# Attention with a gated convolution: the row of reciprocals turned by VectorE, another start and another end

## The chip, the core and the metric

The kernel runs on one core of a Trainium2 chip. The metric is the time on the device, in microseconds (us), of one execution; the kernel before was timed in three runs. A core has five engines that work from queues of their own and wait for each other by semaphores: TensorE (PE, matrix products; its weight loads are listed as PEld), VectorE (DVE), ScalarE (ACT), GpSimd (POOL) and SyncE (SP), which in this kernel issues every DMA transfer. Matrix products land in PSUM, everything else lies in SBUF.

## The reference, cut to what matters

```python
# B, C = 4, 128; 384 x 32 positions, so N = 12288 queries per batch
kv_pool = kv.reshape(B, H // 4, 4, W // 4, 4, C).mean(axis=(2, 4))   # 768 keys per batch
k = v = kv_pool.reshape(B, -1, C) @ w_sr
s = (q @ k.transpose(0, 2, 1)) / sqrt(C)
a = exp(s - s.max(-1));  a /= a.sum(-1) + 1e-09
x = a @ v                                                            # (B, N, C)
gate = sigmoid(sum_k conv_w[k] * xp[:, k:k + N])                     # five causal taps along N
out = (gate * (x @ w_val)) @ w_out
```

The weights `w_val`, `w_out` and `conv_w` arrive as float64 and are turned into float32 on the chip.

## The kernel before, in words

The queries are cut into groups of 512 (`GQ`), 24 for a batch and 96 in all, and a group into four tiles of 128 queries (`NT = 4`). The keys of a batch come in 16 pieces of 384 KB; a piece holds the 16 values that belong to each of 48 keys (`PC = 48`), and `pool_kv` sums them with one `tensor_reduce` on VectorE. Five buffers hold pieces (`AHEAD = 5`).

A tile's work is one step `t` of the main loop, in a hand-written order (the program switches its scheduler to manual, so each engine's instructions stand as the code is written). `score` forms 128 x 768 scores as three products for each half of the keys, with keys and queries split into a high and a low part (`kh`, `kl`, `qh`, `ql`), one tile ahead and in one of three pairs of PSUM banks. `row_max` (VectorE), `expo` (ScalarE, which also sums the row into column `j` of the tile `z`), `p_hi` (ScalarE) and one step later `p_lo` (VectorE) make a high and a low half-precision part of the probabilities. `p_lo` frees the bank pair. In most tiles a DMA transpose (`pt<-hl`) turns the parts; in a group's last tile, TensorE turns them (`turn`, L299). The last batch turns every tile of its even groups by DMA. Two groups later `av_part` multiplies them with the values: 18 products for a group, 7, 2, 3 and 6 in its four steps. `g_x` (VectorE) scales the result with the row of 1/z, which has been spread over all partitions (`rb`), and writes `x`. GpSimd makes four of the convolution's taps and adds them up (`g_conv`, L360 and L369), also subtracts for `ql` (L237), and copies the four values that the next group's `x` needs from the one before (L346). `g_tanh`, `g_val`, `g_h`, `g_out` and `g_evac` finish a group three and more groups behind.

The row of 1/z comes about so. `z` is a 128 x 128 tile of zeros with four columns in use. `norm_reciprocal` (L276, VectorE) inverts the four columns in step `j == 0` of the next group. `norm_turn` (L279) turns the whole tile by a TensorE transpose into the one bank `misc()`. In step `j == 1`, `norm_store` copies four rows of it to SBUF (L286, VectorE) and SP stores these 2 KB to DRAM (`rd<-r`, L287). At the end of step `j == 3`, `norm_rows` (L292) reads them back, broadcast over 128 partitions (`rb<-rd`). `g_x` uses `rb` one group later.

Before the loop stand the loads and sums of the first batch's keys, two projections by `w_sr` (L133, half of the keys each), and the scores of one tile. The weights' load (`load_moe`) is issued after the ninth piece, and its 14 VectorE instructions are strewn over the loop's steps from `t = 3`. Behind the loop stands the end, for the last groups `n1` (the last) to `n5`: `n2` and `n1` are convolved by VectorE alone (`conv_dve`), `n1` in two halves of 256 columns.

## Time and profile before

| | before |
|---|---|
| median of 3 runs | 1077.52 us (1075.18 to 1078.14) |
| profiled execution | 1078.68 us, of which the profile's span is 1076.9 us |
| mean granted TensorE clock | 0.996 |
| busy, us | PE 1038.4, PEld 706.5, DVE 919.5, ACT 903.7, POOL 865.2 |
| chain that ended last | PE 89%, DVE 5%, ACT 2%, DMA 2% |
| DMA queues | 92.7% of 16 engines' span, 220.25 MB |

The span begins with the first instruction on the core and ends with the last; some 2 us of the execution lie outside it. A busy share is a mean over the whole span, and the first 50 us and the last 25 us differ from the middle. A row of the timeline gives start, duration, engine, line, operation, what is written from what is read, and in brackets the idle time before it with what ended it. On SP the duration is that of issuing a transfer, not of its landing.

### The profile page before, as it was taken

The page shows a single profiled execution, that of the slowest core. Times are in us where ns is not written, and L with a number is a line of the kernel's source. Part 1 is how long each engine was busy: PE and PEld are TensorE (multiplying, and loading weights), DVE is VectorE, ACT ScalarE, POOL GpSimd, SP SyncE. Part 2 cuts the span into 40 slices and gives each one's busy share as a digit, 9 for nine tenths or more (in the row PEclk, how much of TensorE's full clock was granted, in tenths as well). Part 3 has the DMA queues.
Part 4 walks back from the last instruction along what each step waited for, and adds up shares of the span by engine and source line. Part 5 has one row for each costly group of instructions (what it writes and reads, how often), then busy time and mean ns, then how long its engine had stood idle before and what let it go on. Part 6 is the DMA issues. An engine that isn't in the chain of part 4 may idle for free.

```text
span 1076.9 us, 16475 instructions
## 1 busy us (share of the span) xinstructions
PE 1038.4 (96%) x5102; PEld 706.5 (66%) x5102; DVE 919.5 (85%) x1290; ACT 903.7 (84%) x1659; POOL 865.2 (80%) x948
## 2 busy tenths in 40 slices
PE   1899999999999999999999999999999999999996
PEld 0666666666666666666676666666666666666663
DVE  6888989898888898988888989898888888888885
ACT  1788888888888888888888888888888988888882
POOL 0178888888888888888888888888887888888882
PEclk9999999999999999999999999999999999999999
DMA  7699999998889999999689999997899999999994
GB/s 285 115 237 215 214 225 234 200 192 190 182 186 234 226 222 224 220 214 188 156 182 221 248 216 219 235 218 177 174 203 191 200 209 218 206 194 212 201 178 120
DMA packets 505527, 220.25 MB, mean 205 GB/s; under 512 B 471520, under 2 KB 472288, under 8 KB 505440
## 3 DMA queue, kind: packets, MB, share of 16 engines
q1 hardware_dynamic: 505440, 219.20, 92.7%
q8 instruction: 41, 0.67, 0.2%
q14 instruction: 46, 0.38, 0.1%
HBM read 75.83 MB, written 25.36 MB: 94 GB/s over the span
## 4 chain that ended last, share of the span: by engine, by line
PE 89%; DVE 5%; ACT 2%; DMA 2%; issue 1%; POOL 0%; SPq 0%; DVEq 0%; ACTq 0%
PE s L251 36%; PE av L333 32%; PE m L389 7%; PE m L399 7%; PE s L299 5%; DMA kvt<-in_kv 2%; DVE nm L257 1%; PE m L279 1%; ACT s L269 1%; ACT hl L316 1%; DVE hl L320 1%; DVE pt L320 1%; DVE pool L120 0%; DVE x L350 0%; PE m L176 0%
## 5 line engine op out<-in xcount | busy, mean ns | idle before, releaser
L333 PE MATMUL av<-pt,vh 128*128 128x512 f16 x1140 | 387.1, 381 | 0.0
L369 POOL TENSOR_TENSOR sum<-sum,tap 128x512 f32<-128x512 f32 x282 | 360.3, 1278 | 22.1
L257 DVE TENSOR_REDUCE nm<-s 128x1 f32<-128x768 f32 x384 | 363.9, 948 | 2.8 <-PE s L251 2.8
L269 ACT ACTIVATE s<-s,nm 128x768 f32<-128x768 f32 x300 | 262.0, 873 | 88.7 <-DVE nm L257 80.0
L360 POOL TENSOR_SCALAR tap<-x,wm 128x512 f32<-128x512 f32 x376 | 253.4, 693 | 78.1 <-DVE x L350 76.8
L320 DVE SCALAR_TENSOR_TENSOR hl<-s,hl 128x768 f16<-128x768 f32 x300 | 284.8, 949 | 21.4 <-ACT hl L316 21.1
L251 PE MATMUL s<-kh,qh 128*128 128x384 f32 x768 | 252.9, 410 | 6.0 <-DVE hl L320 2.3
L316 ACT ACTIVATE hl<-s 128x768 f16<-128x768 f32 x300 | 243.0, 810 | 9.1
L333 PEld LDWEIGHTS <-vh 128*128 128x128 f16 x1164 | 113.5, 98 | 173.6 <-issue 81.5
L333 PE MATMUL av<-pt,vl 128*128 128x512 f16 x570 | 216.0, 379 | 0.0
L251 PE MATMUL s<-kh,ql 128*128 128x384 f32 x768 | 198.0, 339 | 0.0
L251 PE MATMUL s<-kl,qh 128*128 128x384 f32 x768 | 197.7, 338 | 0.0
L237 POOL TENSOR_TENSOR ql<-q,qh 128x512 fp32r<-128x512 f32 x96 | 122.0, 1271 | 93.3 <-ACT qh L233 92.5
L251 PEld LDWEIGHTS s<-kh,qh 128*128 128x128 f32 x768 | 132.4, 192 | 51.1 <-PE m L279 4.4
L251 PEld LDWEIGHTS s<-kl,qh 128*128 128x128 f32 x768 | 140.5, 189 | 0.5 <-DVE kl L146 0.5
L251 PEld LDWEIGHTS s<-kh,ql 128*128 128x128 f32 x768 | 139.8, 189 | 0.0
L394 DVE SCALAR_TENSOR_TENSOR h<-th,m 128x512 f32<-128x512 f32 x94 | 64.7, 688 | 69.0 <-PE m L389 63.4
L369 POOL TENSOR_TENSOR sum<-tap,tap 128x512 f32<-128x512 f32 x94 | 120.3, 1280 | 0.0
L350 DVE SCALAR_TENSOR_TENSOR x<-av,down,rb 128x512 f32<-128x512 f32 x95 | 71.3, 751 | 44.5 <-POOL ql L237 30.5
L333 PEld LDWEIGHTS <-vl 128*128 128x128 f16 x582 | 57.2, 98 | 76.6 <-issue 53.6
L399 PE MATMUL m<-h,wm 128*128 128x512 f32 x188 | 96.8, 597 | 1.2 <-DVE h L394 1.2
L389 PE MATMUL m<-x,wm 128*128 128x512 f32 x188 | 96.1, 592 | 0.0
(68 smaller groups left out, 1001.9 us busy)
## 6 DMA issues: line engine op xcount, KB each, us to landing
kvt<-in_kv SPq DMA_DIRECT2D x64, 384.0 KB
rb<-rd SPq DMA_DIRECT2D x96, 256.0 KB
q<-in_q SPq DMA_DIRECT2D x47, 512.0 KB
out<-o SPq DMA_DIRECT2D x46, 512.0 KB
pt<-hl SPq DMA_TRANSPOSE x192
rd<-r SPq DMA_DIRECT2D x96, 2.0 KB
out<-o SPq DMA_DIRECT2D x3, 256.0 KB
q<-in_q SPq DMA_DIRECT2D x2, 256.0 KB
```

The lines of the kernel that those rows point to most:

```text
L237: nc.gpsimd.tensor_tensor(out=g.ql, in0=g.q, in1=g.qh.bitcast(F32), op=ALU.subtract)
L251: nc.tensor.matmul(s[:, h, :HALF], a[:, sl], k[:, h * HALF:(h + 1) * HALF], start=(i == 0), stop=(i == 2))
L257: nc.vector.tensor_reduce(out=nm, in_=g.s[j], axis=AX.XY, op=ALU.max, negate=True)
L269: nc.scalar.activation(out=halves(g.pf[j]) if on_pe(g, j) else g.s[j], in_=g.s[j], func=AF.Exp, bias=g.nm.pop(j), accum_out=g.z[:, j:j + 1])
L316: nc.scalar.activation(out=part(g, j, 0), in_=g.s[j], func=AF.Copy, scale=2.0 ** 15)
L320: nc.vector.scalar_tensor_tensor(out=part(g, j, 1), in0=g.s.pop(j), scalar=2.0 ** 15, in1=part(g, j, 0), op0=ALU.mult, op1=ALU.subtract)
L333: nc.tensor.matmul(out, g.st[v][:, k * P:(k + 1) * P], g.pt[:, j0:j1, a * NCH + k], start=(i == 0), stop=(i == len(AV_ORDER) - 1))
L350: nc.vector.scalar_tensor_tensor(out=g.x[:, HALO + c0:HALO + c1], in0=av, scalar=g.st["down"], in1=g.rb[:, c0:c1], op0=ALU.mult, op1=ALU.mult)
L360: eng.tensor_scalar(out=g.tap[k], in0=src, scalar1=w, scalar2=1.0, op0=ALU.mult, op1=ALU.mult)
L369: nc.gpsimd.tensor_tensor(out=s, in0=acc, in1=g.tap[k], op=ALU.add)
L389: nc.tensor.matmul(m, wval, g.x[:, HALO + c0:HALO + c1], start=True, stop=True)
L399: nc.tensor.matmul(m, wout, h, start=True, stop=True)
```

## The change: what it does

Three things change.

1. **The row of 1/z.** `norm_turn` leaves TensorE. VectorE turns four blocks of 32 x 32 of `z` (now 128 x 32) straight into the SBUF tile `r`, 32 x 128, of which four rows are stored as before; the copy out of PSUM goes. Reciprocal, four transposes and the store now stand together in step `j == 0`, behind `p_lo(prev)`; the reciprocal stood ahead of it. The broadcast read `norm_rows` stands in step `j == 2` ahead of `p_lo(prev)`, where it stood at the end of step `j == 3`.
2. **The start.** The weights are loaded first of all and converted at once. Pieces 0, 2, 4, 6, 8 and 10 are summed by GpSimd in four halvings (`pool_halving`). The keys are projected in three parts (keys 0 to 383, 384 to 671, 672 to 767), and the scores of tiles 0, 1 and 2 against the first half of the keys are written ahead of the second projection, their other half behind the last.
3. **The end.** `conv_mixed` gives two of the five taps to ScalarE; the order of the last groups' products is another, and PSUM banks are used in pairs.

```diff
-    zs = [const.tile([P, P], F32, name=f"z{i}") for i in range(3)]
+    zs = [const.tile([P, BLOCK], F32, name=f"z{i}") for i in range(3)]
...
+    def pool_halving(st, i):
+        t = st.pop(("kv", i)).rearrange("c (k s) -> c k s", s=RR)
+        n = RR // 2
+        while n:
+            if n == 1:
+                to = st["pool"][:, i * PC:(i + 1) * PC].rearrange("c (k s) -> c k s", s=1)
+            else:
+                to = kvp.tile([C, PC, n], F32, name=f"half{n}", bufs=1)
+            nc.gpsimd.tensor_tensor(out=to, in0=t[:, :, :n], in1=t[:, :, n:2 * n], op=ALU.add)
+            t, n = to, n // 2
...
-    def norm_turn(g, m):
-        nc.tensor.transpose(m[:, :P], g.z, ident)
-        g.rm = m[:NT, :P]
+    def norm_turn(g):
+        g.r = small.tile([BLOCK, P], F32, name="r")
+        for i in range(0, P, BLOCK):
+            nc.vector.transpose(out=g.r[:, i:i + BLOCK], in_=g.z[i:i + BLOCK])
...
-        nc.vector.tensor_copy(out=r, in_=g.rm)
-        nc.sync.dma_start(out=g.rd, in_=r)
+        nc.sync.dma_start(out=g.rd, in_=g.r[:NT])
...
+        late = [product(k) for k in range(TAPS - 2, TAPS)]
         s = work.tile([C, GQ], F32, name="fast")[:, :c1 - c0]
         nc.vector.tensor_scalar_mul(out=s, in0=g.x[:, c0:c1], scalar1=cwt[:, 0:1])
-        for k in range(1, TAPS):
+        for k in range(1, TAPS - 2):
...
+        for t in late:
+            nc.vector.tensor_tensor(out=s, in0=s, in1=t, op=ALU.add)
...
+    convert = load_moe()
     for i in range(AHEAD):
         load_kv(0, st, i)
...
+    by_pool = (1, 3, 5, 7, 9, 11)
+    ends = {PIECES // 2: slice(0, HALF), PIECES - 2: slice(HALF, NK - 2 * PC),
+            PIECES: slice(NK - 2 * PC, NK)}
+    for step in convert:
+        step()
+    for i in range(1, PIECES + 1):
+        (pool_halving if i in by_pool else pool_kv)(st, i - 1)
...
+        if low and (i == PIECES - 1 or i == PIECES - 3):
+            low()
+        if i in ends:
+            project(st, ends[i], misc())
+            high, low = split_keys(st, ends[i])
+            high()
+        if i == PIECES - 3:
+            for j in first:
+                score(at(0), j, (0,))
...
-        if last and j == 0:
-            norm_reciprocal(last)
-        if last and j == 1:
-            norm_store(last)
+        if last and j == 2:
+            norm_rows(last)
         drip()
         if prev:
             p_lo(prev, (j - 1) % NT)
...
         if last and j == 0:
-            norm_turn(last, misc())
+            norm_reciprocal(last)
+            norm_turn(last)
+            norm_store(last)
...
-        if last and j == 3:
-            norm_rows(last)
```

Three places show what moves. The first is VectorE's queue in the middle of the program, from a group's `g_x` (`x<-av,down,rb`) to the next group's `h`; `nm` is the row maximum, `pt` and `hl` are the results of `p_lo`, `z_102` one of the three `z`. Before:

```order
L350 SCALAR_TENSOR_TENSOR x<-av,down,rb 128x512
L257 TENSOR_REDUCE nm<-s 128x1
L276 RECIPROCAL z_102<-z_102 128x4
L320 SCALAR_TENSOR_TENSOR pt<-s,pt 128x768
L257 TENSOR_REDUCE nm<-s 128x1
L286 COPY r<-m 4x128
L320 SCALAR_TENSOR_TENSOR hl<-s,hl 128x768
L394 SCALAR_TENSOR_TENSOR h<-th,m 128x512
```

Now:

```order
L364 SCALAR_TENSOR_TENSOR x<-av,down,rb 128x512
L271 TENSOR_REDUCE nm<-s 128x1
L334 SCALAR_TENSOR_TENSOR pt<-s,pt 128x768
L290 RECIPROCAL z_102<-z_102 128x4
L296 STREAM_TRANSPOSE r<-z_102 32x32 x4
L271 TENSOR_REDUCE nm<-s 128x1
L334 SCALAR_TENSOR_TENSOR hl<-s,hl 128x768
L419 SCALAR_TENSOR_TENSOR h<-th,m 128x512
```

Reciprocal and transposes stand between `p_lo` of the last group's last tile and the row maximum of the group's second tile; the copy is gone.

The second is SP's queue for one group in the same stage, from its DMA transposes on. Before:

```order
L324 DMA_TRANSPOSE pt<-hl 128x24x128
L324 DMA_TRANSPOSE pt<-hl 128x12x128
L292 DMA rb<-rd 128x512
L117 DMA kvt<-in_kv 128x768
L413 DMA out<-o 128x1024
L287 DMA rd<-r 4x128
L222 DMA q<-in_q 128x1024
```

Now:

```order
L338 DMA_TRANSPOSE pt<-hl 128x24x128
L338 DMA_TRANSPOSE pt<-hl 128x12x128
L118 DMA kvt<-in_kv 128x768
L301 DMA rd<-r 4x128
L438 DMA out<-o 128x1024
L235 DMA q<-in_q 128x1024
L306 DMA rb<-rd 128x512
```

The read `rb<-rd` of a group used to stand behind the next pair of DMA transposes; it stands now ahead of them, two or fewer instructions behind the store that it waits for.

The third is VectorE's queue at the start, from the first piece on (`big` is the first step of the values' scaling). Before:

```order
L120 TENSOR_REDUCE pool<-kvt 128x48 x13
L146 SCALAR_TENSOR_TENSOR kl<-s,kh 128x384
L120 TENSOR_REDUCE pool<-kvt 128x48 x3
L146 SCALAR_TENSOR_TENSOR kl<-s,kh 128x384
L257 TENSOR_REDUCE nm<-s 128x1 x2
L162 TENSOR_REDUCE big<-vt 128x1
```

Now, behind the 14 instructions of the conversion, of which the last is the first row here:

```order
L97 TENSOR_TENSOR wm<-rest 128x261
L121 TENSOR_REDUCE pool<-kvt 128x48 x7
L158 SCALAR_TENSOR_TENSOR kl<-m,kh 128x384
L121 TENSOR_REDUCE pool<-kvt 128x48 x2
L158 SCALAR_TENSOR_TENSOR kl<-m,kh 128x288
L121 TENSOR_REDUCE pool<-kvt 128x48
L158 SCALAR_TENSOR_TENSOR kl<-m,kh 128x96
L271 TENSOR_REDUCE nm<-s 128x1 x2
L174 TENSOR_REDUCE big<-vt 128x1
```

VectorE sums ten pieces in place of sixteen, after the conversion; the sum of the last piece stands behind the low part of keys 384 to 671.

More of the change, by code (lines that the diff above doesn't have):

```diff
@@ L18 @@
 GQ = 512
+BLOCK = 32
 NT = GQ // P
@@ L130, in key_tiles, with project, split_keys @@
         st["vt"] = keys.tile([C, NK], F32, name="vt", bufs=1)
-    def project(st, h, m):
-        nc.tensor.matmul(m[:, :HALF], wsr, st["pool"][:, h * HALF:(h + 1) * HALF],
-                         start=True, stop=True)
-        st["m"] = m[:, :HALF]
-    def split_keys(st, h):
-        sl = slice(h * HALF, (h + 1) * HALF)
+    def project(st, sl, m):
+        m = m[:, :sl.stop - sl.start]
+        nc.tensor.matmul(m, wsr, st["pool"][:, sl], start=True, stop=True)
+        st["m"] = m
+    def split_keys(st, sl):
         m = st.pop("m")
@@ L211, in setup_steps @@
         steps = [lambda i=i: piece(i) for i in range(PIECES + 1)]
-        steps += [lambda h=h: project(st, h, misc()) or split_keys(st, h) for h in range(2)]
+        steps += [lambda sl=sl: project(st, sl, misc()) or split_keys(st, sl)
+                  for sl in (slice(0, HALF), slice(HALF, NK))]
         return steps + value_steps(st)
@@ L243, in halves, with score @@
         return a.rearrange("p (h k) -> p h k", h=2)
-    def score(g, j):
+    def score(g, j, part=range(2)):
         sl = slice(j * P, (j + 1) * P)
         kh, kl = g.st["kh"], g.st["kl"]
-        s = bank_pair()
+        if j not in g.s:
+            g.s[j] = bank_pair()[:, :, :HALF]
         for i, (a, k) in enumerate(((g.qh, kh), (g.qh, kl), (g.ql, kh))):
-            for h in range(2):
-                nc.tensor.matmul(s[:, h, :HALF], a[:, sl], k[:, h * HALF:(h + 1) * HALF],
+            for h in part:
+                nc.tensor.matmul(g.s[j][:, h], a[:, sl], k[:, h * HALF:(h + 1) * HALF],
                                  start=(i == 0), stop=(i == 2))
-        g.s[j] = s[:, :, :HALF]
     def row_max(g, j):
@@ L371, in g_conv, with conv_mixed, product @@
         g.gate = acc
-    def conv_dve(g, c0=0, c1=GQ):
+    def conv_mixed(g, c0, c1):
+        def product(k):
+            t = work.tile([C, GQ], F32, name=f"tap{k}", bufs=1 if k < TAPS - 1 else 2)
+            t = t[:, :c1 - c0]
+            nc.scalar.activation(out=t, in_=g.x[:, k + c0:k + c1], func=AF.Copy,
+                                 scale=cwt[:, k:k + 1])
+            return t
+        late = [product(k) for k in range(TAPS - 2, TAPS)]
         s = work.tile([C, GQ], F32, name="fast")[:, :c1 - c0]
         nc.vector.tensor_scalar_mul(out=s, in0=g.x[:, c0:c1], scalar1=cwt[:, 0:1])
-        for k in range(1, TAPS):
+        for k in range(1, TAPS - 2):
             nc.vector.scalar_tensor_tensor(out=s, in0=g.x[:, k + c0:k + c1],
@@ L458, in attn_moe_kernel @@
     load_pair(at(2), at(3))
-    score(at(0), 0)
+    score(at(0), 0, (1,))
     g_qh(at(1))
@@ L477, in attn_moe_kernel @@
             steps += setup_steps(cur.b + 1, states[cur.b + 1])
-        if t == 3:
-            trickle += convert
         if nxt:
-            score(nxt, (j + 1) % NT)
+            score(nxt, (j + 1) % NT, (1,) if t + 1 in first else range(2))
         if mg and j == 1:
@@ L541, in attn_moe_kernel, with pair_of @@
     cuts = ((0, half), (half, GQ))
-    def bank():
-        return bank_pair()[:, 0]
-    norm_reciprocal(n1)
-    av_part(n2, 0)
-    norm_turn(n1, misc())
+    def pair_of(width):
+        both = bank_pair()
+        return both[:, 0, :width], both[:, 1, :width]
+    for i in range(NT):
+        av_part(n2, i)
     n4.th = g_tanh(n4.gate)
@@ L552, in attn_moe_kernel @@
     p_lo(n1, NT - 1)
+    norm_reciprocal(n1)
+    norm_turn(n1)
     norm_store(n1)
     store_pair(n5)
[L555 to L556 removed]
     norm_rows(n1)
+    avs = pair_of(half)
+    av_range(n1, avs[0], 0, len(AV_ORDER), 0, NT // 2)
     n4.m = g_val(n4, misc())
+    av_range(n1, avs[1], 0, len(AV_ORDER), NT // 2, NT)
     new_x(n2, n3, nc.scalar.copy)
     g_x(n2, n2.av)
+    gate2 = conv_mixed(n2, 0, GQ)
+    n2.th = g_tanh(gate2)
+    m2, o2 = pair_of(GQ)
+    g_val(n2, m2)
+    new_x(n1, n2, nc.scalar.copy)
+    g_x(n1, avs[0], *cuts[0])
     h4 = g_h(n4.th, n4.m)
[L562 removed]
     n4.m = g_out(h4, misc())
     out_tile(n4)
+    gates = [conv_mixed(n1, *cuts[0])]
     g_evac(n4, n4.m)
     store(n4)
[L567 to L587 removed]
+    g_x(n1, avs[1], *cuts[1])
+    m3, o3 = pair_of(GQ)
+    g_val(n3, m3)
+    g_out(g_h(n2.th, m2), o2)
+    n3.th = g_tanh(n3.gate)
+    ms = pair_of(half)
+    g_val(n1, ms[0], *cuts[0])
+    gates.append(conv_mixed(n1, *cuts[1]))
+    out_tile(n2)
+    g_evac(n2, o2)
+    store(n2)
+    g_out(g_h(n3.th, m3), o3)
+    g_val(n1, ms[1], *cuts[1])
+    n1.th = work.tile([C, GQ], F32, name="th")
+    ths = [g_tanh(gate, n1.th[:, c0:c1]) for gate, (c0, c1) in zip(gates, cuts)]
+    g_evac(n3, o3)
     store(n3)
[L589 to L591 removed]
+    for th, m, o, c in zip(ths, ms, pair_of(half), cuts):
+        g_evac(n1, g_out(g_h(th, m), o), *c)
         store(n1, *c)
```

47 lines of the change are left out of this document (7 added, 40 removed).

## The prediction

> **What bounds the kernel now.** I read the page's shares first, then a table of stretches, then who TensorE waits for.
>
> ```profile
> PE 1038.4 (96%) x5102; PEld 706.5 (66%) x5102; DVE 919.5 (85%) x1290; ACT 903.7 (84%) x1659; POOL 865.2 (80%) x948
> 10.00:20.00 10.00, 1.65 (x2) 0.50 (x2) 8.31 (x10) 1.49 (x3) 1.26 (x1) 1.00 1.01 375
> 40.00:50.00 10.00, 6.68 (x40) 5.37 (x39) 10.00 (x20) 8.21 (x16) 1.26 (x1) 1.00 0.59 110
> 100.00:150.00 50.00, 50.00 (x250) 34.27 (x248) 45.12 (x63) 43.77 (x80) 43.53 (x48) 1.00 1.01 225
> PE s L133 <- DVE pool L120: 22.0, 2, 14.2
> ```
>
> The stretches give busy us of PE, PEld, DVE, ACT and POOL, then granted clock, DMA share and GB/s. There are three kernels here. From about 50 to 1050 us TensorE is busy all the time (50.00 of 50) and VectorE nine tenths (45.12). Before that TensorE waits 22.0 us for summed keys, which a saturated DMA brings (375 GB/s); then VectorE is the bound (10.00 of 10 from 40 to 50). Behind it a chain of waits stands at the end. Each part of the change aims at one of the three, so I cost them apart, and a us counts only where its engine is the bound.
>
> **The middle: what a TensorE transpose costs.** The group of transposes has a mean of 273 ns, and 96 of them would be 26.2 us. But matmuls overlap, so I read start to start, at one place with the transpose and one without:
>
> ```profile
> L279 PE MATMUL m<-ident,z 128*128 128x128 f32 x96 | 26.2, 273 | 0.6 <-DVE vl L188 0.6
> 144.57 0.59 PE L333 MATMUL av<-pt,vh 128*128 128x512 f16 x2
> 145.00 0.27 PE L279 MATMUL m<-ident,z 128*128 128x128 f32 x1
> 145.47 0.51 PE L251 MATMUL s<-kl,qh 128*128 128x384 f32 x2
> 147.04 0.38 PE L333 MATMUL av<-pt,vl 128*128 128x512 f16 x1
> 147.82 0.51 PE L251 MATMUL s<-kl,qh 128*128 128x384 f32 x2
> 143.63 1.53 PE av L333 x7
> 154.25 1.53 PE av L333 x7
> ```
>
> From the second last `av` product to the second pair of score products it is 145.47 - 144.57 = 0.90 us with the transpose and 147.82 - 147.04 = 0.78 without. The transpose costs 0.12 us of TensorE's time. A group takes 154.25 - 143.63 = 10.62 us, so it becomes 10.50. The first three batches have 72 groups, some 70 of them at this pace: 70 x 0.12 = **8.4 us**, if nobody else needs more than 10.50. VectorE and SP are the ones to test.
>
> **VectorE** loses a copy and gets four transposes:
>
> ```profile
> 134.75 0.27 DVE L286 COPY r<-m 4x128 f32<-4x128 f32 x1
> 134.95 0.95 DVE L320 SCALAR_TENSOR_TENSOR hl<-s,hl 128x768 f16<-128x768 f32 x1
> 136.69 0.69 DVE L394 SCALAR_TENSOR_TENSOR h<-th,m 128x512 f32<-128x512 f32 x1 [0.80 <-PE m L389]
> L276 DVE RECIPROCAL z<-z 128x4 f32<-128x4 f32 x96 | 16.0, 167 | 0.0
> L169 DVE TENSOR_SCALAR diag<-ident,up 128x128 f32<-128x128 f32 x4 | 1.5, 363 | 0.0
> ```
>
> The copy took 134.95 - 134.75 = 0.20 us of the queue. No transpose on VectorE is in the trace. Its nearest rows are the reciprocal with 4 elements (0.17 us) and an SBUF tile of 128 elements (0.36); 32 elements lie near the lower, so about 0.20, or some 0.12 to the next start since neighbours overlap. Four take 0.48, and up to 0.2 more because they depend on the reciprocal: the group grows by about 0.4 us, with bounds of 0.3 and 4 x 0.36 - 0.20 = 1.2. VectorE is busy 45.12/50 x 10.62 = 9.6 us a group, so 10.0 of 10.50. What is late is the row maximum of the second tile and its `p_lo`; the 0.80 us that VectorE idles ahead of `h` take it in. At 1.2 it would need 10.8.
>
> **SP** gets a wait. The store of 1/z and its read back used to lie on either side of the DMA transposes:
>
> ```profile
> 135.80 0.28 SPq L287 DMA_DIRECT2D rd<-r  x1
> 139.19 5.95 SPq L324 DMA_TRANSPOSE pt<-hl  x2
> 145.23 0.86 SPq L292 DMA_DIRECT2D rb<-rd  x1
> 146.14 0.43 SPq L117 DMA_DIRECT2D kvt<-in_kv  x1
> 1047.53 0.43 SPq L287 DMA_DIRECT2D rd<-r  x1
> 1048.45 5.19 SPq L324 DMA_TRANSPOSE pt<-hl  x2
> 1054.63 0.32 SPq L287 DMA_DIRECT2D rd<-r  x1
> 1057.19 0.32 SPq L292 DMA_DIRECT2D rb<-rd  x1
> 10.40 5.39 DMA kvt<-in_kv
> ```
>
> Now the read follows the store, and everything behind it on SP waits until the store has landed: the next two DMA transposes, then keys, queries and outputs. SP's round is 5.2 to 5.95 (transposes) + 0.43 + 0.86 + some 0.3 of gaps = 6.8 to 7.5 us, plus the store's way. Lower bound of that: the last store, issued at 1054.63 and read at 1057.19, 2.5 us. Upper bound: a transfer in the loaded queue of the start, 5.4. The round is 9.3 to 12.9; it fits into 10.50 while the store takes under 3.0 to 3.7. I take 3, since only 2 KB go out and only one piece of keys lies ahead. Some lateness is free: transposes issued by 145.14 feed products at 154.25. What I take for SP is nothing.
>
> **The last batch** is not TensorE's alone:
>
> ```profile
> 853.66 2.69 POOL L360 TENSOR_SCALAR tap<-x,wm 128x512 f32<-128x512 f32 x4 [0.80 <-DVE x L350]
> 863.96 2.69 POOL L360 TENSOR_SCALAR tap<-x,wm 128x512 f32<-128x512 f32 x4 [0.81 <-DVE x L350]
> 874.55 2.03 POOL L360 TENSOR_SCALAR tap<-x,wm 128x512 f32<-128x512 f32 x3 [0.81 <-DVE x L350]
> ```
>
> GpSimd's taps, sums, `ql` and halo lead to VectorE's `x` and back to taps. One group takes 10.30 that way, the next, with TensorE's turn in it, 10.59. Only the second can shrink: 12 x 0.12 = **1.4 us** (0, or 2.8 if both do).
>
> **The start.** The last piece and the first row maxima stand so:
>
> ```profile
> 22.67 0.95 DVE L120 TENSOR_REDUCE pool<-kvt 128x48 f32<-128x768 f32 x1 [0.80 <-DMA kvt<-in_kv]
> 28.25 0.96 DVE L257 TENSOR_REDUCE nm<-s 128x1 f32<-128x768 f32 x1 [1.42 <-PE s L251]
> 30.17 0.96 DVE L257 TENSOR_REDUCE nm<-s 128x1 f32<-128x768 f32 x1 [0.96 <-PE s L251]
> 10.84 1.26 POOL L237 TENSOR_TENSOR ql<-q,qh 128x512 fp32r<-128x512 f32 x1 [9.53 <-ACT qh L233]
> 38.00:60.00 22.00, 4.84 (x14) 0.99 0.85 156
> ```
>
> The same bytes come before the last piece, only the weights earlier, so it lands again near 22.7. VectorE's conversion (4.84 us, the last row, for its tiles alone) delays its first sum by some 4.5 us, but it has ten pieces left, 10 x 0.95. GpSimd's row is 2.5 ns an element (1.26 us for 512), so a piece's 384 + 192 + 96 + 48 outputs take 1.8 us and 2.0 with fixed parts, six of them and one `ql` 13.3 us: from about 5 to 20, in time if its strided reads cost no more. Then the new order bites. Nine half-scores on a TensorE that runs at 30.17 - 28.25 = 1.92 us a tile (six halves) need 2.9 us from about 20.4 (the thirteenth piece lands three times 1.05 us, 384 KB at 375 GB/s, ahead of 22.7, and its sum and the low part of the first half come first); the second projection, its parts `kh` and `kl`, and behind `kl` the sum of the last piece come after them, at about 25.1. Add 0.95, the last projection, `kh`, `kl` and three half products: the first row maximum at 27.9 where it was 28.25, the second at 28.9 where it was 30.17. So 1.3 us are won by then. The 4.84 us of conversion go from a VectorE that was full, but ScalarE, 8.21 of 10 there, is next, and the new transposes come in: I take 0.7 more. **2 us**, with bounds of 6 (1.3 and the whole conversion) and -8 (a halving at twice the price, 13.3 us more, less the slack and the sums that VectorE no longer has).
>
> [...]
>
> **The end.** The read of `n2`'s row waited on SP behind two DMA transposes:
>
> ```profile
> 1053.73 4.14 DMA rb<-rd
> 1058.01 0.75 DVE L350 SCALAR_TENSOR_TENSOR x<-av,down,rb 128x512 f32<-128x512 f32 x1 [4.73 <-POOL sum L369]
> 1059.79 3.11 DVE L377 SCALAR_TENSOR_TENSOR fast<-x,wm,fast 128x512 f32<-128x512 f32 x4
> 1072.53 0.42 DVE L394 SCALAR_TENSOR_TENSOR h<-th,s 128x256 f32<-128x256 f32 x1 [0.15 <-ACT th L385]
> 1055.14 1.02 PE L389 MATMUL m<-x,wm 128*128 128x512 f32 x2
> ```
>
> It landed at 1057.87 and `x` began at 1058.01, though the products were done by 1055.14. Ahead of the transposes it is in time, and `x` begins near 1055.1, 2.9 us earlier. The convolution takes 3.4 where it took 0.5 + 3.1 (two adds in place of two fused steps). But SP's next things slip: the last two DMA transposes start near 1050 in place of 1048.45, because the store of 1047.53 must land first, the store of `n1` comes at 1055.2, its read near 1057.8, landing 3.7 later at 1061.4. VectorE, free at 1059.3, waits for it. Then `n1`'s first half (0.5), `h` (0.7), a half convolution (2.1), second half (0.5), `h` (0.7), half convolution (2.1), two `h` (0.7 and 0.4) lead to the last `h` at about 1069, 3.6 us before 1072.53. **3.6 us**, with bounds of 1 (the row later still) and 6.5 (no wait for it).
>
> **Sum.** 8.4 + 1.4 + 2 + 3.6 = 15.4. The profiled execution took 1078.68 us, its span 1076.9; 1.2 above the median of 1077.52. 1078.7 - 15.4 = 1063.3, and on the median's footing **1062 us**.
>
> **Rivals.** (1) The transpose is worth its whole 273 ns: 82 x 0.27 = 22 in place of 9.8 (82 being the 70 and the 12), 1050 us. The overlap above speaks against it; that loads and stalls around it may go too speaks for it. (2) VectorE or the start gives back: transposes near 0.36 us make a group 10.6 to 10.8 and the middle wins nothing, which leaves 2 + 3.6: 1072 us; or GpSimd is late by 8 us at the start: 1070 us. For it: VectorE's 9.6 us and POOL's strided reads; against: the idle 0.80. (3) **Slower**: SP becomes the bound. If the store takes 4.5 us in the key-loading groups, the round is 7 + 4.5 = 11.5, 1.0 over, in 16 groups of three batches; less the 6 us of slack in each batch, 3 x 10 = 30 us: 1092 us. It decides from 3.7 us on. For it: DMA share 1.01 in that stretch; against: the 2.5 us near the end.
>
> [...]
>
> **Chances.** Forecast 0.67 (1055 to 1068), rival 1 0.08, rival 2 0.17, rival 3 0.08. The range of 1054 to 1073 holds the forecast and rival 2. About 0.3% (3 us) can be told from no change here. Faster takes the forecast, rival 1 and most of rival 2: 0.88; same, its upper end: 0.04; slower: 0.08.
>
> **What would show it.** No L279 on TensorE and a group at 10.50 (middle right); 10.62 with VectorE full, or DMA transposes that start later from group to group with TensorE waiting for `pt` (rivals 2 and 3). In the last batch 10.30 and 10.48 in turn. The first row maximum near 27.9, and fewer idle us of TensorE before 50. At the end `x` of `n2` right behind its products, and VectorE waiting for `n1`'s row. Wrong outright: a middle that is no shorter though TensorE stays full.

## The result: slower, and the profile after

| | before | after |
|---|---|---|
| median of 4 runs | 1077.83 us (1075.18 to 1078.55) | 1085.42 us (1085.28 to 1086.45) |
| profiled execution, span | 1078.68, 1076.91 us | 1085.54, 1083.73 us |

The ratio is 1.0075, with a 95% interval of 1.0060 to 1.0091: 0.8% slower, where 1.4% faster was forecast. To see where the time went I cut each span at the starts of four row maxima on VectorE, those of tiles 0, 20 (the sixth group), 288 (the last batch's first) and 383 (the last). The runs behind the second row are experiments, explained below.

| kernel | median, us | tile 0 starts at | tile 20 starts at | tiles 20 to 288 | 288 to 383 | 383 to end |
|---|---|---|---|---|---|---|
| before | 1077.83 | 28.25 | 78.96 | 720.32 | 249.03 | 28.60 |
| after | 1085.42 | 31.45 | 83.05 | 720.16 | 252.46 | 28.05 |
| e1_row_only | 1081.61 | 27.89 | 80.76 | 719.76 | 252.88 | 26.58 |
| e2_start_only | 1081.16 | 31.40 | 79.77 | 722.21 | 248.85 | 28.38 |
| e3_end_only | 1078.46 | 27.82 | 78.58 | 720.39 | 249.00 | 28.94 |
| e4_no_turn | 1065.52 | 27.40 | 77.76 | 712.94 | 246.73 | 26.52 |
| e5_one_transpose | 1104.72 | 28.23 | 78.28 | 735.85 | 260.33 | 29.99 |
| e9_one_store | 1073.35 | 28.01 | 79.64 | 717.08 | 246.73 | 26.78 |
| e14_row_late | 1066.81 | 27.23 | 78.17 | 711.55 | 246.74 | 28.69 |
| e16_four_late | 1083.30 | 27.23 | 80.54 | 719.70 | 252.87 | 27.43 |
| e11_after_one | 1078.21 | 31.25 | 80.55 | 719.21 | 246.58 | 30.77 |
| e15_row_late_end | 1065.27 | 27.38 | 78.21 | 711.53 | 246.68 | 27.18 |

The span grew by 6.8 us: the start lost 4.1, the middle won 0.2 where 8.4 were expected, the last batch lost 3.4 and the end won 0.6. (Each row of the table is one trace. With the same code a start or an end varies from trace to trace by up to 1.7 us, the middle by a few tenths.) The changed kernel's page has these shares:

```profile
PE 1039.6 (96%) x5008; PEld 694.4 (64%) x5008; DVE 975.2 (90%) x1573; ACT 918.0 (85%) x1667; POOL 879.7 (81%) x972
```

VectorE's busy time rose by 56 us. Two stretches of the changed kernel (us from and to, length, busy us of PE, PEld, DVE, ACT and POOL, granted clock, DMA share, GB/s); before, the first had 375 GB/s and the second 45 us of VectorE's:

```profile
10.00:20.00 10.00, 2.34 (x3) 0.79 (x3) 4.58 (x5) 1.49 (x3) 8.48 (x15) 1.00 0.84 294
150.00:200.00 50.00, 50.00 (x247) 33.58 (x246) 47.91 (x74) 44.49 (x82) 42.88 (x47) 1.00 0.99 219
```

And its chain of waits, in the middle and in the last batch:

```profile
137.00 1.53 PE av L347 x7
147.63 1.53 PE av L347 x7
...
847.73 1.53 PE av L347 x7
869.00 1.53 PE av L347 x7
```

A group of the middle still takes 147.63 - 137.00 = 10.63 us (10.61 over many), with its TensorE transpose gone, and a pair of groups in the last batch takes 21.27 where it was 20.89. VectorE's queue in one group of the changed kernel's middle (start, duration, engine, line, operation, idle time in brackets):

```profile
137.80 0.17 DVE L290 RECIPROCAL z<-z 128x4 f32<-128x4 f32 x1
138.00 0.84 DVE L296 STREAM_TRANSPOSE r<-z 32x32 f32<-32x32 f32 x4
138.78 0.90 DVE L271 TENSOR_REDUCE nm<-s 128x1 f32<-128x768 f32 x1
139.71 0.96 DVE L334 SCALAR_TENSOR_TENSOR hl<-s,hl 128x768 f16<-128x768 f32 x1
140.59 0.68 DVE L419 SCALAR_TENSOR_TENSOR h<-th,m 128x512 f32<-128x512 f32 x1
...
144.10 0.96 DVE L334 SCALAR_TENSOR_TENSOR hl<-s,hl 128x768 f16<-128x768 f32 x1 [0.23 <-ACT hl L330]
...
146.01 0.75 DVE L364 SCALAR_TENSOR_TENSOR x<-av,down,rb 128x512 f32<-128x512 f32 x1
```

From the reciprocal to the next row maximum it is 138.78 - 137.80 = 0.98 us, and the 0.80 us ahead of `h` are gone. The 0.23 us for ScalarE's high part were there before too. What holds the round shows when TensorE is laid beside it. In the changed kernel:

```profile
140.73 0.30 PEld L266 LDWEIGHTS s<-kh,qh 128*128 128x128 f32 x2 [0.34 <-DVE hl L334]
145.53 0.38 PE L347 MATMUL av<-pt,vh 128*128 128x512 f16 x1
```

And before, where the `p_lo` of the same step is the prediction's row at 134.95:

```profile
136.67 0.70 PE L251 MATMUL s<-kh,qh 128*128 128x384 f32 x2
142.04 0.75 DVE L350 SCALAR_TENSOR_TENSOR x<-av,down,rb 128x512 f32<-128x512 f32 x1
```

In the changed kernel `p_lo` ends at 139.71 + 0.96 = 140.67, and TensorE's next scores, which need the PSUM bank that it frees, start 0.06 us later. From there TensorE works on to the last `av` product, which ends at 145.91, and `x` starts 0.10 behind it. Then VectorE works with hardly a pause from `x` to the next such `p_lo`: 10.61 - (146.01 - 140.67) = 5.27 us. The round is a loop of VectorE's part and TensorE's, one after the other. Before, the same `p_lo` ended at 135.90, 0.77 us ahead of the scores at 136.67, and VectorE's part was 10.62 - (142.04 - 135.90) = 4.48 us. So the transposes made VectorE's part 0.79 us longer, where some 0.7 were free. Neither engine's busy time tells of it: TensorE is listed as busy for 50.00 us of 50 before and after, though it waits. In the kernel before, the weight loads of the scores wait 2.8 us in all for this `p_lo`, 5 times. Who waits for whom in the changed kernel (us in total, times, longest):

```profile
PEld s L266 <- DVE hl L334: 27.8, 73, 2.2
PEld L347 <- DMA pt<-hl: 0.5, 2, 0.3
```

From SP's own list of waits:

```profile
SPq L306 <- DMA rd<-r: 141.9, 85, 3.9
```

SP does wait for its store, 142 us in all, but hardly anyone waits for what SP issues late (`pt`, 0.5 us).

### The profile page after: what moved, and what is told of

The parts are those of the page before. It is cut to its first block, busy times and chain, and to the rows that moved or that the text cites. A ratio compares the mean times of both kernels' runs of the same rounds, so it can differ in the third digit from the quotient of the medians.

```text
span 1083.7 us, 16406 instructions
## 1 busy us (share of the span) xinstructions
PE 1039.6 (96%) x5008; PEld 694.4 (64%) x5008; DVE 975.2 (90%) x1573; ACT 918.0 (85%) x1667; POOL 879.7 (81%) x972
## 4 chain that ended last, share of the span: by engine, by line
PE 76%; DVE 14%; ACT 5%; POOL 2%; issue 2%; DMA 1%; DVEq 0%; ACTq 0%; POOLq 0%
PE s L266 31%; PE av L347 27%; PE m L424 6%; PE m L414 6%; PE s L313 4%; DVE nm L271 4%; DVE hl L334 2%; ACT s L283 2%; DVE x L364 2%; ACT hl L330 2%; DVE r L296 2%; POOL ql L250 1%; DVE pt L334 1%; DMA kvt<-in_kv 1%; PE m L147 1%
## 5 line engine op out<-in xcount | busy, mean ns | idle before, releaser
L271 DVE TENSOR_REDUCE nm<-s 128x1 f32<-128x768 f32 x384 | 359.9, 937 | 2.2 <-PE s L266 2.2
L330 ACT ACTIVATE pt<-s 128x768 f16<-128x768 f32 x84 | 68.2, 812 | 36.0 <-PE s L313 36.0
```

The lines of the kernel that those rows point to most:

```text
L271: nc.vector.tensor_reduce(out=nm, in_=g.s[j], axis=AX.XY, op=ALU.max, negate=True)
L330: nc.scalar.activation(out=part(g, j, 0), in_=g.s[j], func=AF.Copy, scale=2.0 ** 15)
```

## Experiments

**The three parts, each alone.** The edit is in each case one part of the diff above on the kernel before; in the third, TensorE still turns 1/z.

```diff
 e1_row_only     + part 1 (VectorE turns 1/z, early read of the row)
 e2_start_only   + part 2 (weights first, GpSimd's sums, half scores)
 e3_end_only     + part 3 (new end)
```

> The kernel before with the first part of the change alone: 1/z turned by four VectorE transposes, store in step 0, broadcast read in step 2; start and end as before. Theory V (VectorE's four transposes, 0.84 us, stand ahead of the second tile's row maximum and close a round of VectorE and ScalarE): a group of the first three batches stays at 10.6 us and a pair of the last batch's groups goes from 20.9 to 21.3, so 1080 to 1082 us. Theory S (SP's wait for the store is what takes the gain): the same totals, but the DMA transposes start later from group to group. Theory P (nothing but the start is wrong in the changed kernel): the middle at 10.50, 1068 us.

> The kernel before with the second part alone: weights first and converted at once, six pieces summed by GpSimd, three projections, half-scores ahead. Theory C (conversion beside GpSimd's sums takes 6.5 us, releases the buffers late and starves the DMA; the half-scores on a slow TensorE then hold up the second projection): first row maximum at 31.4 us where it was 28.25, 3 to 4 us longer, 1081 us. Rival: the loss in the changed kernel comes from VectorE's transposes in the first groups and the start alone is even, 1078 us.

> The kernel before with the third part alone: two taps on ScalarE, new order of the last groups; the row of n2 is read as late as before. Theory E (in the changed kernel the end lost its gain because VectorE's fused steps ran beside GpSimd's sums, 1.65 us each in place of 0.75): here the convolution of n2 begins after 1058 us, when GpSimd is nearly done, its steps take 0.75 us and the end is 1 to 3 us shorter, 1075 to 1077 us. Rival (the new order itself is no shorter): 1077 to 1079 us.

Measured: 1081.61 us, ratio 1.0042 [1.0027, 1.0056]; 1081.16, 1.0033 [1.0020, 1.0047]; 1078.46, 1.0008 [0.9999, 1.0018]. The first two lose on their own and the third wins nothing; 0.0042 + 0.0033 + 0.0008 = 0.0083 against 0.0075 for all three. Part 1 alone has the middle (719.76) and the last batch (252.88) of the changed kernel, so the loss there is part 1's.

**Nobody turns 1/z.** Part 1 with its four transposes taken out, so that `x` is scaled by wrong values; the place of the store and of the early read stay, so that SP still waits.

```diff
-        for i in range(0, P, BLOCK):
-            nc.vector.transpose(out=g.r[:, i:i + BLOCK], in_=g.z[i:i + BLOCK])
...
-        nc.sync.dma_start(out=g.rd, in_=g.r[:NT])
+        nc.sync.dma_start(out=g.rd, in_=g.z[:NT])
```

> As the kernel with the first part alone, but nobody turns 1/z: neither TensorE nor VectorE, no copy; the store takes four rows of z as they lie, so the output is scaled by wrong rows. Store and read stand where the change puts them. Theory V: TensorE's 0.12 us a group is won in the first three batches, 10.5 us a group, and 0.1 to 0.3 a pair in the last, 1066 to 1069 us. Theory S: the wait on SP is still there, a group stays at 10.6 and the total near 1078.

Measured: 1065.52 us, 0.9893 [0.9875, 0.9910], slightly under its forecast. Its chain has two groups in 20.98 us, 10.49 each:

```profile
131.23 1.53 PE av L331 x7
152.21 1.53 PE av L331 x7
```

SP waits as long as ever, by its list of waits:

```profile
SPq L290 <- DMA rd<-z: 153.2, 96, 4.0
```

So the four transposes cost 16 us (1081.61 - 1065.52), and SP's wait is not what holds the changed kernel.

**One transpose in place of four.** An instruction on a tile of 128 x 32 turns its four blocks at once, in 0.21 us. The rows of 1/z then lie in partitions 0 to 3, 32 to 35 and so on, and four small stores put them together.

```diff
-        for i in range(0, P, BLOCK):
-            nc.vector.transpose(out=g.r[:, i:i + BLOCK], in_=g.z[i:i + BLOCK])
+        nc.vector.transpose(out=g.r, in_=g.z)
...
-        nc.sync.dma_start(out=g.rd, in_=g.r[:NT])
+        for b in range(0, P, BLOCK):
+            nc.sync.dma_start(out=g.rd[:, b:b + BLOCK], in_=g.r[b:b + NT])
```

> As the first part alone, but 1/z lies in a tile of 128x32 and ONE transpose on VectorE turns all four blocks at once; four stores of 4x32 then bring the rows to their places. Nothing is left out. Theory V (the group is held by VectorE's chain: four transposes one after the other, 0.84 us, in the loop between VectorE and ScalarE): one transpose takes about 0.2 us, VectorE gets 0.6 us back, the group falls to TensorE's 10.50 as in the run without a turn, and the time is near that run's: 1066 us (1064 to 1069). Rival P (an instruction costs by its blocks: four blocks in one cost as much as four): it takes 0.8 us, group 10.61, 1081 us. Rival S (four small stores in SP's queue in place of one delay the DMA transposes): TensorE waits for pt, over 1070 us.

Measured: 1104.72 us, 1.0246 [1.0219, 1.0272]. The instruction takes 0.21 us, as the theory on VectorE says, but SP becomes the bound, as the last rival says. From its groups of instructions (busy us, mean ns):

```profile
L282 DVE STREAM_TRANSPOSE r<-z 128x32 f32<-128x32 f32 x96 | 20.4, 212 | 3.3
```

From SP's queue in two groups that load keys, and from the list of waits:

```profile
142.21 1.33 SPq L288 DMA_DIRECT2D rd<-r  x4
146.15 6.45 SPq L325 DMA_TRANSPOSE pt<-hl  x2
153.70 1.35 SPq L288 DMA_DIRECT2D rd<-r  x4
```

```profile
PE av L334 <- DMA pt<-hl: 23.3, 26, 2.3
```

SP's round is 153.70 - 142.21 = 11.5 us there, and TensorE waits for `pt` 26 times. This is the forecast's third rival, with another trigger.

**One store, then the late read.** `e9_one_store` stores all 32 rows at once and uses four of them. `e14_row_late` also moves the read of the row back behind the DMA transposes, where the kernel before has it. `e16_four_late` is the fourth corner: the four transposes with the late read.

```diff
 e9_one_store (on e5_one_transpose)
-        for b in range(0, P, BLOCK):
-            nc.sync.dma_start(out=g.rd[:, b:b + BLOCK], in_=g.r[b:b + NT])
+        nc.sync.dma_start(out=g.rd.rearrange("c (b p) -> b c p", p=BLOCK), in_=g.r)
 e14_row_late (on e9_one_store), e16_four_late (on e1_row_only)
-        if last and j == 2:
-            norm_rows(last)
...
+        if last and j == 3:
+            norm_rows(last)
```

> The single transpose of 128x32 again, but its whole tile (32 rows of 1/z, of which four are used) goes out with one store in place of four. Start and end are those of before. What the four-store run left open: its VectorE had time (922 us busy, one transpose 0.21 us), yet a group took 11.4 us and SP issued two DMA transposes (5.84 us), four stores (1.33), keys (0.86) and waited for the stores to land, one after the other. Theory S (SP's round was the bound there, not VectorE): with one store SP's round is that of the four-transpose run again, TensorE is the bound, the group takes 10.50 us in the first three batches, and the time is that of the run without a turn: 1066 us (1064 to 1069). Rival (the transposed tile or a second effect of it costs, whatever the stores): a group stays over 10.6 and the time over 1075 us.

> One transpose of 128x32 and one store, as in the run that took 1073.35 us, but the read of the row of 1/z stands where the kernel before has it: behind the two DMA transposes of the group, in the fourth tile. Nothing else moves. In the run with the early read most groups took 10.47 us, but some of those that load keys took 10.8 to 12, with TensorE waiting up to 0.85 us for pt. Theory R (there SP has no time left: store 0.54, its way of 2.7, read 0.33, transposes 5.9 to 7.1, keys 0.9, in one after the other; the read ahead of the transposes makes them wait for the store): with the read behind them these groups take 10.47 too, and TensorE does not wait for pt: 3 to 5 us less in the three batches, and an end 2 us longer, since n2 waits for its row again: 1070 us (1067 to 1072). Rival (the larger store or the DMA load itself delays the transposes): the long groups stay, 1073 to 1076 us.

> The fourth corner of a square: four transposes of 32x32 as in the change, with the read of the row behind the DMA transposes as before. Start and end are those of before. The other corners: four and early read 1081.61, one and early read 1073.35, one and late read 1066.81 us. Theory V (four transposes fill VectorE's queue, so that a group takes 10.6 us whatever SP does): the late read brings nothing in the middle, a group stays at 10.6, the last batch at 252 to 253 us, and since n2's row is read late again the end grows by 2 us: 1080 to 1084 us. Rival A (the two prices simply add: late read minus 6.5): 1075 us.

| | read early, as in the change | read late, as before |
|---|---|---|
| four transposes | 1081.61, 1.0042 [1.0027, 1.0056] | 1083.30, 1.0064 [1.0048, 1.0081] |
| one transpose, one store | 1073.35, 0.9962 [0.9950, 0.9975] | 1066.81, 0.9897 [0.9879, 0.9915] |

With four transposes the place of the read changes nothing in the middle (719.76 and 719.70 us) or the last batch; with one it is worth 717.08 - 711.55 = 5.5 us. The two prices do not add: VectorE's hides SP's. `e9_one_store` missed both of its forecasts. Most of its groups take 10.47 us; some, mostly of those that load keys or right behind them, take 0.3 to 1.0 us more than in `e14_row_late`, up to 11.5. In one of these TensorE's queue has this row, and SP's the rows behind it:

```profile
155.21 0.38 PE L333 MATMUL av<-pt,vh 128*128 128x512 f16 x1 [0.85 <-DMA pt<-hl]
```

```profile
142.34 0.54 SPq L287 DMA_DIRECT2D rd<-r  x1
145.23 0.33 SPq L292 DMA_DIRECT2D rb<-rd  x1
145.67 7.11 SPq L324 DMA_TRANSPOSE pt<-hl  x2
152.83 0.92 SPq L118 DMA_DIRECT2D kvt<-in_kv  x1
153.84 0.54 SPq L287 DMA_DIRECT2D rd<-r  x1
156.77 0.33 SPq L292 DMA_DIRECT2D rb<-rd  x1
```

The transposes that TensorE waits for were issued at 145.67, behind a read that came 145.23 - 142.34 = 2.9 us after its store. At the next store, with nothing else to issue, SP sits 156.77 - 153.84 = 2.9 us before it may go on to read and transpose. With the late read nobody on TensorE waits for `pt`. The chain of `e14_row_late`, then VectorE's queue:

```profile
131.54 1.53 PE av L333 x7
142.01 1.53 PE av L333 x7
```

```profile
142.81 0.17 DVE L277 RECIPROCAL z<-z 128x4 f32<-128x4 f32 x1
143.01 0.21 DVE L282 STREAM_TRANSPOSE r<-z 128x32 f32<-128x32 f32 x1
143.15 0.91 DVE L258 TENSOR_REDUCE nm<-s 128x1 f32<-128x768 f32 x1
143.98 0.95 DVE L320 SCALAR_TENSOR_TENSOR hl<-s,hl 128x768 f16<-128x768 f32 x1
145.55 0.69 DVE L394 SCALAR_TENSOR_TENSOR h<-th,m 128x512 f32<-128x512 f32 x1 [0.62 <-PE m L389]
```

A group takes 10.47 us in step, and VectorE idles ahead of `h` again (0.62). Over the rounds between 80 and 240 us, the median time from that `p_lo` to the scores is 0.59 us here, 0.65 in `e4_no_turn`, 0.77 before, and 0.06 in the three kernels with four transposes (the changed one, `e1_row_only` and `e16_four_late`). VectorE's part is 4.51, 4.47, 4.47 and 5.27 us.

**The whole change with one transpose.** The same edit, with the one store, in the changed kernel.

> The whole changed kernel with one edit: 1/z is turned by one transpose of 128x32 with one store, in place of four transposes. If the four transposes are what made the change slower in the middle and in the last batch, this wins back 8.4 us of the first three batches and some 4 to 6 of the last one, and only the start (1 to 4 us) and the end (1 to 2) stay behind the single transpose alone: 1070 us (1067 to 1073). If the middle's loss has another cause in the changed kernel: 1080 to 1086 us.

Measured: 1078.21 us, 1.0001 [0.9987, 1.0016], outside both forecasts. Against the changed kernel the last batch wins 5.9 us and the start 2.5, but the middle only 1.0 (with the early read, TensorE's `av` waits for `pt` again, 4.4 us in its list of waits) and the end loses 2.7: its `n1` waits for DMA transposes that are held up by the store (`pt`, 2.5 us on TensorE).

**The start.** Two edits on `e2_start_only` undo one thing each; the third builds on the first.

```diff
 e6_conv_back: weights loaded at the fourth piece, converted in the loop as before
-    convert = load_moe()
-    for step in convert:
-        step()
 e12_no_pool_sums: VectorE sums all pieces
-    by_pool = (1, 3, 5, 7, 9, 11)
+    by_pool = ()
 e13_no_half (on e6_conv_back): no scores ahead of the second projection
-    first = range(3)
+    first = ()
```

> As the second part alone (the new start, TensorE still turns 1/z), but the weights are loaded at the fourth piece of keys and converted step by step inside the loop, as before; GpSimd's sums and the early half products stay. Theory C (the loss at the start comes from the conversion: beside GpSimd's sums it takes 6.5 us, VectorE's sums of keys come late, the buffers of the pieces come free late and the DMA queue runs empty): the first row maximum falls from 31.4 to 27 to 28.5 us, the time to 1076 to 1079 us. Rival H (the loss comes from the half products on a TensorE at low clock and from sums that GpSimd brings late): the first row maximum stays at 30 to 31.5, the time at 1080 to 1082 us.

> The new start alone (TensorE turns 1/z, the end of before), but no piece of keys is summed by GpSimd: VectorE sums all of them, after the conversion of the weights. Theory L (VectorE's steps with two SBUF inputs, and its fast steps, wait for the GpSimd instruction that is running): without GpSimd's sums the 14 conversion steps take 4.2 to 4.9 us in place of 6.8, and the longest TENSOR_TENSOR among them 0.4 to 0.5 us in place of 1.1 to 1.2. Rival (the conversion is slow there by itself, by the loads that run or its place): it stays near 6.5 us. The time is not the point: the sums are VectorE's alone, so the first row maximum comes at 29 to 33 us.

> The new start alone with the conversion back in the loop (the run in which the first row maximum came at 29.58), and no half products of scores ahead of the second projection: all score products come after the keys are done, as before. GpSimd's sums stay. Theory H (the rest of the loss, 29.58 against 28.25, comes from the half products and the projection behind them on a TensorE at low clock): the last piece's sum moves from 26.69 to 24 or earlier and the first row maximum to 27 to 28.3. Rival D (keys arrive late since GpSimd holds each piece for over 2 us and the loads wait for its buffer): the last sum stays behind 26 and the first row maximum at 29 or later.

The medians are 1081.13 us, 1.0028 [1.0017, 1.0040], and, single runs, 1078.90 and 1077.88. The first row maximum comes at 29.58, 31.82 and 28.90, against 31.40 in `e2_start_only` and 28.25 before. So the early conversion costs 1.8 us of the 3.15 there, each figure from one trace. The other two steps, 0.7 for the half scores and 0.65 that stay, are too small to be told apart: in the runs that have the start of before, the first row maximum lies between 27.17 and 28.41. `e6_conv_back` and `e13_no_half` thus fall between their two forecasts of the first row maximum, and `e6_conv_back` wins nothing of the total. What stretches the conversion shows in two rows of VectorE's queue, first in the changed kernel, then in `e12_no_pool_sums`, where GpSimd sums nothing:

```profile
4.83 1.20 DVE L97 TENSOR_TENSOR rest<-rest 128x261 int32<-128x261 int32 x1
8.90 1.10 DVE L97 TENSOR_TENSOR wm<-rest 128x261 f32<-128x261 f32 x1
```

```profile
4.99 0.43 DVE L96 TENSOR_TENSOR rest<-rest 128x261 int32<-128x261 int32 x1
7.94 0.43 DVE L96 TENSOR_TENSOR wm<-rest 128x261 f32<-128x261 f32 x1
```

The 14 steps take 4.78 us without GpSimd (from 3.59 to 8.37) and 6.6 beside it (from 3.43 to 10.00). But the first row maximum is no earlier without GpSimd's sums. The conversion stands ahead of VectorE's sums in any case, the five buffers stay full and the load waits for them (SP 4.3 us for VectorE's sums in the changed kernel, 3.5 of them at once): 312 GB/s from 10 to 20 us in `e12_no_pool_sums`, 294 in the changed kernel, 352 with the conversion back in the loop and no half scores. In that last run SP waits for GpSimd to free a piece:

```profile
SPq L117 <- POOL half L133: 4.6, 5, 1.9
```

Why its first row maximum is not earlier than before's stays open: GpSimd takes 2.38 us for a piece, VectorE 0.95, but no run with the conversion in the loop gave these pieces back to VectorE. Most of what the start loses comes back, since VectorE need not convert later: `e2_start_only` is 3.15 us late at tile 0 and 0.8 at tile 20. `e6_conv_back` is 0.3 late there, and both stumble once more, each at the change to another batch, over one instruction (last section). Their medians lie 3.4 and 3.7 us above the kernel before, these two traces 2.3 and 1.9; the rest stays open.

**The end.** `e7_end_order` changes the order of two products in part 3; `e8_one_and_end` and `e10_one_and_end` are `e5_one_transpose` and `e9_one_store` with that end, and `e15_row_late_end` is `e14_row_late` with it, the last group alone reading its row early.

```diff
-    g_out(g_h(n3.th, m3), o3)
     g_val(n1, ms[1], *cuts[1])
+    g_out(g_h(n3.th, m3), o3)
```

> As the third part alone (the new end, TensorE still turns 1/z), but the value products of the second half of n1 stand ahead of the output product of n3 in TensorE's queue. Theory Q (the last h waited 1.73 us for these products because they stood behind the output product, which waits for h of n3): the wait goes and the end is 1.0 to 1.7 us shorter than in the third part alone, 1076.7 to 1077.5 us. Rival F (the end is held by VectorE's fused steps, stretched beside GpSimd's sums, which come before): the wait only moves and the time stays at 1078.5 us.

> The single transpose of 128x32, the start of before, and the new end with the order of the run on the end's queue. Nothing is left out. If V and Q hold: the middle of the single transpose (group 10.50), and an end some 0 to 1.5 us shorter than that of the single transpose alone, since in that one the row of n2 is already read early: 1064 to 1067 us. If the fused steps beside GpSimd's sums hold the end (F): 0.5 to 2 us longer than the single transpose alone, 1067 to 1070 us.

> As the single transpose with one store, but with the new end, the value products of the second half of n1 ahead of the output product of n3; the start is that of before. The run of the end's order alone was 0.7 us shorter than before while its n2 waited 1.82 us for the row of 1/z, which here is read early. Theory Q: from the last row maximum to the end some 26 us, 0.5 us less than in the single transpose with one store (26.5 as in the run without a turn): 1065 us, or the same within 1.5 us. Rival F (the fused steps of n2, begun earlier, fall beside GpSimd's sums and wait for them): 27.5 to 28.5 us from the last row maximum to the end, 1067 us.

> The same with the read behind the transposes in all groups but the last, where n2's row is read ahead of them, and with the new end (value products of the second half of n1 ahead of the output product of n3); the start is that of before. Theory R for the middle, and an end of 26 to 28 us from the last row maximum in place of 28.6: 1068 us (1065 to 1070). If the rival to R holds: 1072 to 1075 us.

Measured: 1077.68, 1.0002 [0.9993, 1.0012]; 1103.90, 1.0254 [1.0226, 1.0281]; 1072.77, 0.9961 [0.9946, 0.9977]; 1065.27, 0.9888 [0.9869, 0.9908]. The last is the best kernel here, 1.1% faster than before, though its interval overlaps that of `e14_row_late`. `e8_one_and_end` and `e10_one_and_end` missed their forecasts, which had taken a short middle for granted. `e7_end_order` ends 1.1 us earlier behind its last row maximum than `e3_end_only` (27.88 and 28.94), at the low end of the 1.0 to 1.7 expected, and its median is 0.8 lower. The wait for the value products fell from 1.73 to 0.62 us only, and TensorE had a lower clock there: the first output product took 2.08 us where it took 1.12. The same ten us of `e3_end_only`, then of `e7_end_order`:

```profile
1060.00:1070.00 10.00, 4.45 (x11) 1.64 (x10) 8.89 (x18) 4.96 (x11) 0.00 (x0) 1.00 0.14 52
```

```profile
1060.00:1070.00 10.00, 7.23 (x13) 3.01 (x12) 9.20 (x19) 4.26 (x10) 0.00 (x0) 0.66 0.09 31
```

The third figure from the end is the granted clock, 1.00 and 0.66. Why it was lower, no run shows.

The new order is not needed for what the end won: with the order of before and the early read alone the end takes 26.58, 26.52 and 26.78 us (`e1_row_only`, `e4_no_turn`, `e9_one_store`), with the late read 27.04 to 28.69 in seven traces, and in the changed kernel 28.05. In `e8_one_and_end` and `e10_one_and_end` the end (33.5 and 29.2 us) is longer than that of before, because SP is late there and `n1`'s products wait for `pt` (4.0 and 2.2 us). What the fused steps cost shows in the changed kernel's timeline; the first row is GpSimd's:

```profile
1062.70 4.35 POOL L383 TENSOR_TENSOR sum<-sum,tap 128x512 f32<-128x512 f32 x3
1062.72 0.75 DVE L364 SCALAR_TENSOR_TENSOR x<-av,down,rb 128x512 f32<-128x512 f32 x1 [1.29 <-POOL sum L383]
1064.29 3.31 DVE L400 SCALAR_TENSOR_TENSOR fast<-x,wm,fast 128x512 f32<-128x512 f32 x2
1069.11 0.48 DVE L364 SCALAR_TENSOR_TENSOR x<-s,down,rb 128x256 f32<-128x256 f32 x1
1078.27 0.75 DVE L419 SCALAR_TENSOR_TENSOR h<-th,s 128x256 f32<-128x256 f32 x2 [1.73 <-PE s L414]
```

Each of the two fused steps takes 1.65 us where the prediction's row has 3.11 / 4 = 0.78. In `e3_end_only`, where `n2` comes later, they fall behind GpSimd's sums, and the two take 1.54 together.

## Why the prediction was wrong, point by point

The forecast was 15.4 us won and 6.8 were lost. Of these 22.2 us the middle makes 8.2, the start 6.1, the last batch 4.8 and the end 3.0.

**The middle: the term of TensorE was right, the test of VectorE was not.** Taking the transpose off TensorE makes a group 10.47 to 10.49 (forecast 10.50), and tiles 20 to 288 then take 8.8 us less (`e14_row_late`; forecast 8.4). In the changed kernel it is 0.2. The step that failed is "the group grows by about 0.4 us". VectorE's part of the loop grew by 0.79, well within the bounds of 0.3 and 1.2. Priced were transposes at 0.12 to the next start, as neighbours that overlap; they stood 0.21 apart, each starting when the one before was done, and reciprocal and turn took 0.98 us where reciprocal and copy took 0.28. That is 0.7 of the 0.79; the rest is in the row maximum and `p_lo` around them. With it failed "the 0.80 us that VectorE idles ahead of `h` take it in". What could be taken in is the time that `p_lo` was early for the scores, 0.77 - 0.06 = 0.71 us at the old round, and 0.59 at the round of 10.49 that `e4_no_turn` shows. By these figures a growth of 0.4 would have kept the gain; 0.79 kept nothing of it. I had set busy time, 9.6 + 0.4 = 10.0, against 10.50, and by that sum even 0.79 would have fitted. Busy time does not tell that VectorE's part and TensorE's follow each other. The second rival had VectorE take the middle's gain, though by transposes of 0.36 us, and called it 1072; that the last batch, start and end would lose by it was not in its price.

**The last batch.** 1.4 us were to be won; 3.4 were lost. The step "Only the second can shrink" counted TensorE and GpSimd and left VectorE's transposes out of a loop that runs through VectorE's `x`. VectorE is not full there (43.5 us of 50 from 850 to 900), since it has no keys to sum; it waits for TensorE, which the transposes made late:

```profile
899.27 0.75 DVE L364 SCALAR_TENSOR_TENSOR x<-av,down,rb 128x512 f32<-128x512 f32 x1 [0.96 <-PE av L347]
```

That the four transposes are the cause is shown (252.88 with them, 246.73 without, and 246.74 with one), which wait decides in each of the two kinds of groups is not. With one transpose the batch is 2.3 us shorter than before.

**SP: nothing, as taken, but for another reason.** The store's way was about the 3 us that I took (2.9 in `e9_one_store`), and SP waited as described (141.9 us over 85 groups). It cost nothing because the loop through VectorE was later still. Take that cover away and the same wait costs 5.5 us in the middle. The third rival's mechanism is real, and its point of decision lay nearer than the forecast had it.

**The start: 2 us won in the forecast, 4.1 lost.** The step "so it lands again near 22.7" failed: the same bytes do not arrive at the same time if the conversion holds the buffers (375 GB/s became 294). The conversion's 4.84 us were right for itself (4.78) and wrong beside GpSimd (6.6). A halving by GpSimd took 2.38 us a piece, with its gaps, for an estimated 2.0. "0.7 more" for the conversion's absence from the loop was too little (2.3 came back), but the new transposes took 1.8 at the same place (`e1_row_only` at tile 20).

**The end: 3.6 forecast, 0.6 measured.** `x` of `n2` stands right behind its products, as said, and the early read alone does shorten the end (26.58 us in `e1_row_only`). The new order lost that again: the two fused steps took 1.65 each beside GpSimd's sums (1.8 us lost), and the last `h` waits 1.73 us for value products that stand behind another output product. The wait for `n1`'s row, priced in, did not come (its `x` at 1069.11 without idle time). In `e15_row_late_end`, with the order mended, the end is 1.4 us shorter than before, which is no more than the same end varies from trace to trace. The granted clock was 0.94, 0.89 and 0.92 in the last three stretches before (from 1050 us), and 1.00, 1.00 and 0.98 in those of the changed kernel (to 1083).

## What to carry to other kernels

Before work is moved from one engine to another, follow one round from engine to engine: where one engine's part can only start when the other's ends, the two lengths add up (here VectorE's 5.27 us and TensorE's 5.34, gaps included, make the round of 10.61), and busy shares do not tell (50.00 us of 50 on TensorE, 47.91 on VectorE). The room is the time that a result lies ready before it is used, here 0.6 to 0.7 us of 10.6, and what was added cost the distance between starts, 0.21 us for each of the four transposes. Price a small instruction by its count, and look for the form that does all blocks at once: here one transpose of 0.21 us in place of four, with the row read late in both, turned 0.6% slower into 1.0% faster. Where an effect seems free, ask which other delay hides it: SP's wait cost nothing under four transposes and 5.5 us under one.

## What the runs showed of the hardware that was not expected

**A transpose on VectorE cost by the instruction.** One of 32 x 32 took 0.20 us, one of 128 x 32, four times as much, 0.21. Four in a row stand 0.21 us apart, while the row maximum behind the single one starts after 0.14 (143.01 to 143.15). Why the four do not overlap, no run shows.

**Some of VectorE's operations waited for GpSimd's running instruction.** Beside GpSimd's additions, two of VectorE's additions of two SBUF tiles took 1.20 and 1.10 us for 0.43 (another, begun within 0.01 us of one of GpSimd's, kept its 0.43), the fused steps 1.65 for 0.78. Row maxima and `p_lo`, whose scores lie in PSUM, kept their 0.95. One such instruction makes the stumble of the start's runs: a scaling of 128 x 128 on VectorE, once in a batch, which met a GpSimd addition at its beginning (`e2_start_only`, start and duration):

```profile
268.65 1.38 DVE L180 TENSOR_SCALAR diag<-ident,up 128x128 f32<-128x128 f32 x1
269.96 0.94 DVE L333 SCALAR_TENSOR_TENSOR hl<-s,hl 128x768 f16<-128x768 f32 x1
```

The 18 traces have 72 of these scalings. Of those that began while no addition ran, 28 took 0.27 to 0.28 us (in the changed kernel an addition began 0.06 to 0.26 us behind each of its four). The 42 that began while one ran took 0.39 to 0.53, and each ended 0.08 to 0.09 us behind it. The two others, which began 0.04 us ahead of one, took 1.38 and also ended 0.08 behind it. In `e2_start_only` 1.4 us of the run's middle hang on it (tile 91 of the trace is 2.25 us late, tile 89 was 0.9). `e6_conv_back` has the same 1.38 us two changes of batch later, at 785.10. The additions and the fused steps read two SBUF tiles (up to 1.20 and 1.65 us); the row maxima and `p_lo`, which kept their 0.95, read one tile from PSUM; the scaling reads one SBUF tile and a column. What in an instruction makes it wait, no run shows.
